# A planned two-branch attention kernel: other times in its plan, one more row place, output products one place later, another table of order

## The chip, the cores and the metric

The kernel runs on one core of a Trainium2 chip. The metric is the device time of one execution in microseconds. The profiler's records of one execution give the span, the busy times and the waits that are quoted below.

## The reference

Two attention layers A and B (own weights, same input `x` of 2048 tokens x 640 features) are computed and mixed with a gate for each token. Each layer has 32 heads of 20 features and works in 4 segments of 512 tokens: causal softmax attention inside the segment (the mask of -1e9 hides a key from the queries ahead of it), plus a read of a memory `M, z` that the earlier segments have filled.

```python
for s in range(N):
    qs, ks, vs = q[:, :, s], k[:, :, s], v[:, :, s]
    logits = jnp.einsum("bhqd,bhkd->bhqk", qs, ks) * scale + mask
    p = _softmax(logits, axis=-1)
    a_dot = jnp.einsum("bhqk,bhkd->bhqd", p, vs)
    pq = phi(qs)
    a_mem = jnp.einsum("bhld,bhde->bhle", pq, M) / (jnp.einsum("bhld,bhd->bhl", pq, z)[..., None] + 1e-6)
    outs.append(g * a_mem + (1.0 - g) * a_dot)
    pk = phi(ks)
    M = M + jnp.einsum("bhld,bhle->bhde", pk, vs)
    z = z + jnp.einsum("bhld->bhd", pk)
...
return g * (a @ wo_A) + (1 - g) * (b @ wo_B)
```

## The kernel before

The eight pairs of segment and layer are numbered `t` = 0 to 7 (`t // 2` is the segment, `t % 2` the layer). For each `t` there are 8 units of four heads, so 64 units `i = 8 t + u`.

**What a unit does.** `s_unit` multiplies queries with keys on TensorE (line 1207); VectorE then scans each block of scores for its row maximum (line 1194), which frees the bank of PSUM that held the block. The maxima are turned into rows on TensorE (`mrow_unit`, line 1232) and sent by DMA into two spare rows of the query tile, so that `t_unit` (line 1297) gets scores with the maximum already taken off. ScalarE takes the exponential (1289), GpSimd cuts the triangle (1290), and `pv_unit` (1317) multiplies with the values. Scores run two units ahead (`LEAD`).

**Fill work.** Between the units TensorE gets products of 640 x 640 weights in split precision: `job_qk`, `job_v`, `job_o`, all through line 771. Each is a list of matmuls of 64 rows on one half of the array, so that two different pieces of work run side by side on the two halves. `window_jobs(t)` writes the list of products that belong to the window of `t`: the remaining q, k and v of `t`, then the first of the five products in `HEAD` of `t + 1` (q0, k0, q1, k1, q2), then the five output products of `t - 1`, then the rest of `HEAD`. PSUM has eight banks, shared by all.

**From the end of a `t` to its output products.** The last `pv_unit` of a `t` sends its rows to memory (`send_dot`). `reciprocals(t, ...)` loads the denominators and gates: line 1377 multiplies them, line 1382 inverts them in two halves of 1.7 us each on VectorE. `mix` loads five blocks of numerators, multiplies each with the inverse (line 1427 on VectorE or 1428 on GpSimd), adds the transposed memory part (1495), and splits the sum into a high and a low part (1418 on ScalarE, 1420 on VectorE or 1421 on GpSimd). Only then can `job_o(t, ...)` run.

**What sets the order.** All engines get an order written ahead by a planner in the kernel: it simulates the engines with a time for each operation (the numbers in `put("D", 0.605, ...)`, `anyof(... D=(...), G=(...))` and `dma(us, ..., lat=...)`), and emits each instruction when its simulated start comes. On the chip each engine runs its list strictly in that order. A time in the plan is thus no wait on the chip; it decides what stands before what, and `anyof` takes the engine with the smaller simulated load. `RULES` holds, for each unit, eight numbers of the planner (order of S and T units, share of the fill, how long units are put off, and so on).

**Rows.** `big` is a pool of 28 places of 128 x 512 f32 in SBUF (`NBIG`) for inputs, split products, probabilities and results. In the last `t`, `fin_unit` used one tile `fin_tmp` of its own.

## Time and profile before

| | |
|---|---|
| Median of 3 runs | 1021.28 us (1020.8 to 1024.54) |
| Profiled execution, own time | 1020.24 us |
| Its span, first to last instruction | 1018.2 us |
| TensorE matmul busy | 1000.0 us, 98% |
| TensorE weight load busy | 857.4 us, 84% |
| VectorE (DVE) busy | 773.7 us, 76% |
| ScalarE (ACT) busy | 659.7 us, 65% |
| GpSimd (POOL) busy | 606.0 us, 60% |
| Granted TensorE clock | 1.000 |

PE is TensorE's matmul row and PEld its weight loads; "busy" is the union over both halves of the array, so a stretch in which only one half works counts as busy in full. A wait row names the engine that waits and its line, then what it waited for, then us in total, the number of times and the longest. Windows give the busy time of each engine in a stretch, with the number of its instructions in brackets.

### The profile page before, as it was taken

To read this page: it belongs to the slowest core of one execution; us is meant where nothing else is said; L and a number is where in the kernel's file an instruction comes from. 1 tells how busy PE (TensorE), PEld (TensorE's weight loads), DVE (VectorE), ACT (ScalarE), POOL (GpSimd) and SP (SyncE) were. 2 spreads that over 40 slices of the span, in tenths; PEclk is the share of its full clock that TensorE was granted. 3 is DMA by queue.
4 is the path that set the end of the run, shared out by engine and by line. 5 is a ranking of instruction groups with operands and counts; after the bars stand their busy time and mean duration, and the time that the engine had idled before them with its cause. 6 is when DMAs were issued, how large, how long until landed. Compare 5 with 4: busy or idle time off the path is not lost.

```text
span 1018.2 us, 30838 instructions
## 1 busy us (share of the span) xinstructions
PE 1000.0 (98%) x11260; PEld 857.4 (84%) x11260; DVE 773.7 (76%) x2611; ACT 659.7 (65%) x1342; POOL 606.0 (60%) x1032
## 2 busy tenths in 40 slices
PE   9899999999999999999999999999999999999998
PEld 7898888878897888878898888988889888888876
DVE  5587876976787768885777977788747887789764
ACT  5276767677775677666765657675676667665672
POOL 4365557756566655766645557486564646557561
PEclk9999999999999999999999999999999999999999
DMA  6998888988997788868768497786976979878531
GB/s 222 299 313 263 272 274 288 289 278 254 263 298 195 253 240 265 249 190 258 230 177 290 130 297 231 223 283 185 279 240 179 310 206 275 243 221 242 133 117 54
DMA packets 148886, 241.99 MB, mean 238 GB/s; under 512 B 13216, under 2 KB 46144, under 8 KB 148416
## 3 DMA queue, kind: packets, MB, share of 16 engines
q1 hardware_dynamic: 148736, 240.03, 76.8%
q8 instruction: 89, 1.46, 0.6%
q14 instruction: 61, 0.50, 0.2%
HBM read 150.83 MB, written 94.65 MB: 241 GB/s over the span
## 4 chain that ended last, share of the span: by engine, by line
PE 84%; DMA 6%; DVE 5%; issue 1%; POOL 1%; ACT 1%; SPq 1%; DVEq 0%; ACTq 0%; POOLq 0%
PE bank L771 48%; PE bank L1317 13%; PE bank L1297 7%; PE bank L1207 7%; PE bank L881 3%; PE bank L963 2%; PE bank L923 2%; DMA dots<-row 1%; DVE bank L1194 1%; DVE row L1420 1%; PE bank L1232 1%; DMA kd<-row 1%; DVE row L1427 1%; DMA qd<-row 1%; DMA kst<-kd 1%
## 5 line engine op out<-in xcount | busy, mean ns | idle before, releaser
L1194 DVE CUSTOM_DVE_ANT_0 bank<-bank,tri 128x512 f32<-128x512 f32 (+3 forms) x1024 | 474.4, 519 | 151.5 <-PE bank L1207 118.6
L771 PE MATMUL bank<-row,wh 64*128 64x512 f32 x2308 | 498.4, 403 | 0.5 <-DVE O L898 0.3
L1289 ACT ACTIVATE p<-bank 128x512 f32<-128x512 f32 x576 | 316.5, 599 | 138.0 <-PE bank L1297 108.9
L1290 POOL TENSOR_SCALAR_AFFINE_SELECT p<-p 128x256 f32<-128x256 f32 (+1 forms) x576 | 219.3, 390 | 224.8 <-ACT p L1289 215.6
L771 PEld LDWEIGHTS bank<-row,wh 64*128 64x128 f32 x2308 | 319.7, 185 | 10.9 <-issue 1.2
L771 PE MATMUL bank<-row,wl 64*128 64x512 f32 x1154 | 297.0, 399 | 0.0
L541 POOL TENSOR_TENSOR wl<-wst,wh 128x640 fp32r<-128x640 f32 x115 | 180.2, 1573 | 65.4 <-ACT wh L539 64.8
L1207 PE MATMUL bank<-kst,qst 60*128 60x384 f32 (+3 forms) x1024 | 177.9, 317 | 4.6 <-DMA kst<-kd 2.8
L1297 PE MATMUL bank<-qst,kst 62*128 62x128 f32 (+3 forms) x1024 | 179.4, 316 | 3.0 <-DVE mx L1194 2.6
L771 PE MATMUL bank<-wvh,row 64*128 64x320 f32 x1280 | 179.8, 315 | 1.1 <-DVE mx L1194 1.1
L771 PEld LDWEIGHTS bank<-row,wl 64*128 64x128 f32 x1154 | 175.0, 186 | 4.1 <-issue 0.2
L771 PEld LDWEIGHTS bank<-wvh,row 64*128 64x128 f32 x1280 | 147.9, 185 | 3.0 <-DVE mx L1194 1.3
L1194 DVE DVE_READ_ACCUMULATOR2_ANT mx<- 128x1 f32 x1024 | 143.4, 140 | 0.0
L1297 PEld LDWEIGHTS bank<-qst,kst 62*128 62x128 f32 x1024 | 134.3, 186 | 9.5 <-DVE mx L1194 3.9
L1317 PE MATMUL bank<-p,vst 128*32 128x256 f32 (+3 forms) x1904 | 142.1, 427 | 0.0
L1207 PEld LDWEIGHTS bank<-kst,qst 60*128 60x128 f32 x1024 | 130.9, 186 | 11.8 <-DMA kst<-kd 2.0
L1317 PEld LDWEIGHTS bank<-p,vst 128*32 128x32 f32 x1904 | 57.8, 110 | 83.4 <-issue 62.5
L539 ACT CAST wh<-wst 128x640 fp32r<-128x640 f32 x119 | 86.1, 741 | 31.6 <-PE bank L771 14.6
L771 PE MATMUL bank<-wvl,row 64*128 64x320 f32 x640 | 100.7, 311 | 0.0
L771 PEld LDWEIGHTS bank<-wvl,row 64*128 64x128 f32 x640 | 80.3, 185 | 0.1
L516 POOL TENSOR_TENSOR wvl<-wst,wvh 128x640 fp32r<-128x640 f32 (+1 forms) x48 | 64.1, 1338 | 25.4 <-ACT wvh L513 15.7
L1347 ACT COPY row<-bank 128x512 f32<-128x512 f32 x56 | 33.1, 590 | 64.4 <-PE bank L1317 59.6
(117 smaller groups left out, 1204.3 us busy)
## 6 DMA issues: line engine op xcount, KB each, us to landing
qst<-qd SPq DMA_DIRECT2D x128, 240.0 KB
kst<-kd SPq DMA_DIRECT2D x128, 240.0 KB
qd<-row SPq DMA_DIRECT2D x40, 512.0 KB
kd<-row SPq DMA_DIRECT2D x40, 512.0 KB
dots<-row SPq DMA_DIRECT2D x56, 256.0 KB
wst<-wmix SPq DMA_DIRECT2D x35, 320.0 KB
row<-dots SPq DMA_DIRECT2D x42, 256.0 KB
qd<-row SPq DMA_DIRECT2D x40, 256.0 KB
```

The costliest lines, as they stand in the source:

```text
L516: put("G", 0.77 * n, lambda: nc.gpsimd.tensor_tensor(out=wl[:, a:b, :], in0=w3, in1=r32(wh[:, a:b, :]), op=ALU.subtract), end, prio=4)
L539: put("A", 0.625, lambda: nc.scalar.copy(wh, w3), lambda: put(lo_eng, lo_cost, lambda: lo.tensor_tensor(out=wl, in0=w3, in1=r32(wh), op=AL ...
L541: lambda: lo.tensor_tensor(out=wl, in0=w3, in1=r32(wh), op=ALU.subtract), end, prio=3), prio=6)
L771: return nc.tensor.matmul(bank_of, lhsT=w[ROWS[half]], rhs=x_[ROWS[half]], start=start, stop=stop)
L881: return nc.tensor.matmul(pm[:, a - h0:c - h0, :].rearrange("p h e -> p (h e)"), lhsT=r32(pqTs[t, m][ROWS[half], P * n:P * (n + 1)]), rhs= ...
L1194: put("D", w / 960.0 + 0.105, lambda: nc.vector.tensor_tensor_reduce(out=sc[:, off:off + w], in0=sc[:, off:off + w], in1=tri[:, L - w:], s ...
L1207: lane_ops[half].append((mm(w), lambda pair=pair, qb=qb, off=off, w=w, r=r, sc=sc: nc.tensor.matmul(sc[:, off:off + w], lhsT=q[r, pair, P ...
L1289: put("A", 0.483, lambda: nc.scalar.activation(pt, sc, AF.Exp, scale=SCALE), lambda: (bank.give(sc), put("G", 0.15 + 0.105 * len(todo), la ...
L1290: "G", 0.15 + 0.105 * len(todo), lambda: nc.gpsimd.affine_select(out=blocks, in_=blocks, pattern=[[0, len(todo)], [1, P]], base=0, channel ...
L1297: lane_ops[half].append((mm(w), lambda pair=pair, kb=kb, off=off, w=w, r=r, sc=sc: nc.tensor.matmul(sc[:, off:off + w], lhsT=k[r, pair, P ...
L1317: nc.tensor.matmul(po[32 * j:32 * j + 32, P * kb:], lhsT=vst[t % 2][:, kb, h * E1:h * E1 + 32], rhs=pts[i, n, f][0][:, off:off + w], start ...
L1347: either(0.483, lambda: nc.scalar.copy(r32(oT), po), 0.605, lambda: nc.vector.tensor_copy(r32(oT), po), end, 2)
```

## The change

The planner gets other times: VectorE's operations with both inputs in SBUF go from 0.605 to 0.85 or 0.9 us, GpSimd's multiply from 1.25 to 1.4, most loads land 0.2 to 0.4 us sooner in the plan (those of the v weights and the token gates too, not shown below), and the score loads of units 0 and 1 land 1.7 us later than they did in it. `big` gets a 29th place, and `fin_unit` takes its temporary from `big`. `window_jobs` puts the output products behind four products of the next `t` instead of three. Nearly all rows of `RULES` are others. No arithmetic changes: both programs hold 9,732 matmuls and 940 DMAs.

```diff
     RULES = {
-        0: "TSTSTSTSTS 1.010 2.38 0.30 8 0.0 1.6 1",
...
+        0: "TSTSTSTSTS 0.933 2.38 0.30 4 0.0 3.08 1",
...
-    def dma(us, emit, then=None, prio=5, lat=1.1, some=False, issue=0.44):
+    def dma(us, emit, then=None, prio=5, lat=0.9, some=False, issue=0.44):
...
-    NBIG, NWST, NWH, SPARE = 28, 3, 4, 2
+    NBIG, NWST, NWH, SPARE = 29, 3, 4, 2
...
         ahead = [(t + 1, kind, m) for kind, m in HEAD] if t < 7 else []
-        got += ahead[:3]
+        got += ahead[:4]
         if t > 0:
             got += [(t - 1, "o", m) for m in range(KT)]
-        got += ahead[3:]
+        got += ahead[4:]
...
-                out=r32(st), in_=xT[P * k:P * (k + 1), L * s:L * (s + 1)]), landed, prio=need[job_index[2 * s, "q", 0]] - 4 * (s > 0), lat=1.6 if s else 1.1)
+                out=r32(st), in_=xT[P * k:P * (k + 1), L * s:L * (s + 1)]), landed, prio=need[job_index[2 * s, "q", 0]] - 4 * (s > 0), lat=1.2 if s else 1.1)
...
                     dma(0.95, lambda dst=dst, src=rows[half], half=half: nc.sync.dma_start(
-                        out=r32(dst[64 * half:64 * half + 3 * DH, :, :]), in_=r32(src)), done, prio=soon)
+                        out=r32(dst[64 * half:64 * half + 3 * DH, :, :]), in_=r32(src)), done, prio=soon, lat=0.9 if i > 1 else 2.8)
...
         def gates():
-            put("D", 0.605, lambda: nc.vector.scalar_tensor_tensor(
+            put("D", 0.9, lambda: nc.vector.scalar_tensor_tensor(
...
-            out=r32(d), in_=lanes_of(t)[:, DH:DH + 1, :].to_broadcast([H, 4, L])), landed, prio=-1, lat=1.6)
+            out=r32(d), in_=lanes_of(t)[:, DH:DH + 1, :].to_broadcast([H, 4, L])), landed, prio=-1, lat=1.2)
...
-                D=(0.605, lambda: nc.vector.tensor_tensor(out=lo, in0=r32(y), in1=r32(hi), op=ALU.subtract)),
+                D=(0.85, lambda: nc.vector.tensor_tensor(out=lo, in0=r32(y), in1=r32(hi), op=ALU.subtract)),
...
-                D=(0.605, lambda: nc.vector.tensor_tensor(out=r32(y), in0=r32(y), in1=r32(r), op=ALU.mult)),
-                G=(1.25, lambda: nc.gpsimd.tensor_tensor(out=r32(y), in0=r32(y), in1=r32(r), op=ALU.mult)))
+                D=(0.9, lambda: nc.vector.tensor_tensor(out=r32(y), in0=r32(y), in1=r32(r), op=ALU.mult)),
+                G=(1.4, lambda: nc.gpsimd.tensor_tensor(out=r32(y), in0=r32(y), in1=r32(r), op=ALU.mult)))
...
-        dma(0.82, lambda: nc.sync.dma_start(out=r32(y), in_=lanes_of(t)[:, 4 * k:4 * k + 4, :]), landed, prio=0, lat=1.6)
+        dma(0.82, lambda: nc.sync.dma_start(out=r32(y), in_=lanes_of(t)[:, 4 * k:4 * k + 4, :]), landed, prio=0, lat=1.2)
...
-    fin_tmp = Store([sb.tile([P, NB, 4, DH], F32, tag=f"ft{i}", name=f"ft{i}", bufs=1) for i in range(1)])
...
-                def got(tmp):
+                def got(row):
+                    tmp = r32(row[:, :4 * NB * DH]).rearrange("p (n h e) -> p n h e", n=NB, h=4)
...
-                fin_tmp.want(1, got)
+                big.want((F32,), got, prio=1)
```

The order of the instructions shows what that moves. First place: TensorE at the start of the program, where the first scores of unit 0 (line 1207, now 1209) stand among the products for v (`wvh`, 128x320). Before:

```order
L771 MATMUL bank_134<-wvh,row_29_204 128x320
L771 MATMUL bank_136<-row_29_204,wh_145 128x512
L1207 MATMUL bank_137<-kst_84,qst_80 128x512
L1207 MATMUL bank_140<-kst_84,qst_80 128x512
L771 MATMUL bank_134<-wvh,row_8_193 128x320
L923 MATMUL bank_135<-ident,row_232_392 128x64 x2
L771 MATMUL bank_134<-wvh,row_15_196 128x320
L923 MATMUL bank_135<-ident,row_232_392 128x64 x2
L771 MATMUL bank_141<-wvh,row_7_192 128x320
L771 MATMUL bank_134<-wvh,row_20_199 128x320
L771 MATMUL bank_141<-wvh,row_14_195 128x320
L771 MATMUL bank_134<-wvh,row_25_202 128x320
```

Now (lines are two further down):

```order
L773 MATMUL bank_134<-wvh,row_20_198 128x320
L773 MATMUL bank_141<-wvh,row_19_197 128x320
L773 MATMUL bank_134<-wvh,row_25_201 128x320
L773 MATMUL bank_141<-wvh,row_24_200 128x320
L773 MATMUL bank_134<-wvh,row_30_204 128x320
L773 MATMUL bank_141<-wvh,row_29_203 128x320
L773 MATMUL bank_134<-wvl,row_7_191 128x320
L773 MATMUL bank_141<-wvh,row_8_192 128x320
L773 MATMUL bank_134<-wvl,row_14_194 128x320
L773 MATMUL bank_141<-wvh,row_15_195 128x320
L1209 MATMUL bank_137<-kst_84,qst_80 128x512
L1209 MATMUL bank_139<-kst_84,qst_80 128x512
```

The two first scores stood ahead of the product with `row_8` of v; now they stand behind sixteen more products (and four transposes, `ident`). The loads they need (`qst_80`, `kst_84`) stand at the same place in the DMA queue as before. The first score of unit 1 likewise stands twelve matmuls later.

Second place: VectorE at the change to `t` = 7, where the inverse of `t` = 6 is made (L1382, now L1384) and its numerators are multiplied (L1427, now L1429). Before:

```order
L737 TENSOR_TENSOR row_17745_15009<-bank_139,row_17744_15008 128x512
L720 TENSOR_SCALAR bank_138<-bank_138 128x512
L1382 RECIPROCAL row_17623_14935<-row_17623_14935 128x256
L721 TENSOR_TENSOR row_17729_15000<-bank_138,row_17729_15000 128x512
L1382 RECIPROCAL row_17623_14935<-row_17623_14935 128x256
L1468 TENSOR_TENSOR fw_15126<-bank_134,gqd 128x16
L1469 RECIPROCAL fw_15126<-fw_15126 128x16
L1470 TENSOR_TENSOR ft_164<-bank_134,fw_15126 128x320
L1427 TENSOR_TENSOR row_17632_14939<-row_17632_14939,row_17623_14935 128x512
L1427 TENSOR_TENSOR row_17635_14940<-row_17635_14940,row_17623_14935 128x512
L1427 TENSOR_TENSOR row_17641_14942<-row_17641_14942,row_17623_14935 128x512
L1194 ISA bank_139,mx_14991<-bank_139,tri 128x384
```

Now:

```order
L1379 SCALAR_TENSOR_TENSOR row_17688_14937<-row_17688_14937,gcol_132,row_17689_14938 128x512
L723 TENSOR_TENSOR row_17778_14992<-bank_137,row_17778_14992 128x512
L1384 RECIPROCAL row_17688_14937<-row_17688_14937 128x256
L1196 ISA bank_136,mx_14999<-bank_136,tri 128x512
L1196 ISA mx_14999 128x1
L1384 RECIPROCAL row_17688_14937<-row_17688_14937 128x256
L1468 TENSOR_TENSOR fw_15134<-bank_134,gqd 128x16
L1469 RECIPROCAL fw_15134<-fw_15134 128x16
L1470 TENSOR_TENSOR row_17926_15111<-bank_134,fw_15134 128x320
L1429 TENSOR_TENSOR row_17700_14942<-row_17700_14942,row_17688_14937 128x512
L1429 TENSOR_TENSOR row_17706_14944<-row_17706_14944,row_17688_14937 128x512
L1196 ISA bank_138,mx_14999<-bank_138,tri 128x384
```

A scan (L1194, now L1196) has come between the two halves of the inverse, and one of the three multiplications has gone to GpSimd. Over the whole program VectorE has 12 of the 35 multiplications instead of 18, and 16 of the 35 subtractions of line 1420 instead of 18.

Third place: the DMA queue (SP) in the window of `t` = 2, where weight tiles (`wst`) are fetched: `wmix` are the weights of the output products of `t` = 1, `in_b_wk` those of k1 of `t` = 3. Before, end of the five output products:

```order
L1165 DMA qst_82<-qd_99 60x2x512 x2
L1165 DMA kst_86<-kd_107 60x2x512 x2
L550 DMA wst_142<-wmix_131 128x5x128
L1033 DMA row_6379_5392<-part_113 128x512
L750 DMA kd_108<-row_6386_5395 128x2x512
L750 DMA kd_108<-row_6387_5396 128x512
L550 DMA wst_144<-in_b_wk_dram 128x640
L1244 DMA qst_80<-mr_163 2x8x128 x2
L550 DMA wst_143<-in_b_wq_dram 128x640
```

Now, their beginning:

```order
L1167 DMA qst_80<-qd_99 60x2x512 x2
L1167 DMA kst_84<-kd_107 60x2x512 x2
L552 DMA wst_142<-in_b_wk_dram 128x640
L552 DMA wst_143<-wmix_131 128x5x128
L552 DMA wst_144<-wmix_131 128x5x128
L1167 DMA qst_81<-qd_99 60x2x512 x2
L1167 DMA kst_85<-kd_107 60x2x512 x2
L552 DMA wst_142<-wmix_131 128x5x128
L1364 DMA dots_119<-row_6224_5233 128x512
```

The weights of k1 came behind the last block of `wmix`; now they come ahead of the first. The output products begin one product later in each window from `t` = 1 to 6.

## The prediction

> **What bounds the kernel now.** I read the page first, then TensorE's waits, then those of its weight loads.

> ```profile
> span 1018.2 us, 30838 instructions
> PE 1000.0 (98%) x11260; PEld 857.4 (84%) x11260; DVE 773.7 (76%) x2611; ACT 659.7 (65%) x1342; POOL 606.0 (60%) x1032
> ```

> TensorE is the bound, and its work does not change. What a new order can win is the 18.2 us in which no matmul ran, and time in which only one half of the array worked, which counts as busy. TensorE's waits, longest first:

> ```profile
> PE bank L1207 <- DMA kst<-kd: 2.8, 2, 1.7
> PE bank L1297 <- DVE mx L1194: 2.6, 3, 1.3
> PE bank L923 <- DVE mx L1194: 2.1, 1, 2.1
> ...
> PE bank L771 <- DVE mx L1194: 1.1, 1, 1.1
> ...
> PE bank L1207 <- DVE mx L1194: 0.6, 2, 0.4
> PE bank L1207 <- DVE mw L895: 0.4, 1, 0.4
> ```

> One wait is for the first key loads; the others, 6.8 us, are all for VectorE, nearly all for banks that its scans (L1194) had not yet freed. The weight loads say the same, and more of it, since a blocked half shows there while the other half still multiplies:

> ```profile
> PEld bank L1297 <- DVE mx L1194: 3.9, 4, 1.8
> PEld bank L923 <- DVE mx L1194: 2.7, 3, 2.3
> ...
> PEld bank L1207 <- DVE mx L1194: 1.8, 5, 0.7
> ```

> These are 8.4 us against 5.3 of the matmul rows of the same lines: 3.1 us in which a half stood still under a busy mark.

> VectorE is 76% busy on average, so the question is where it is late. I looked for stretches in which it worked without a break and hardly on a scan. The windows of L1194 alone (length, VectorE busy with scans, count):

> ```profile
> 432.60:443.10 10.50, 0.06 (x2) 1.00 0.95 279
> 548.60:558.00 9.40, 0.00 (x0) 1.00 0.93 312
> 695.10:704.50 9.40, 0.00 (x0) 1.00 0.78 213
> 913.10:924.70 11.60, 0.06 (x2) 1.00 1.05 333
> 513.90:520.70 6.80, 0.00 (x0) 1.00 0.81 237
> 571.40:578.10 6.70, 0.00 (x1) 1.00 0.71 255
> ```

> Four stretches of 9.4 to 11.6 us, each where one `t` ends and its inverse and mixing fall on VectorE, and two of 6.7 us. What TensorE lost behind them (window, then PE, PEld, DVE, ACT, POOL busy):

> ```profile
> 514.00:524.00 10.00, 10.00 (x135) 8.35 (x134) 8.27 (x23) 3.46 (x9) 2.90 (x6) 1.00 0.74 223
> 572.00:582.00 10.00, 10.00 (x119) 8.95 (x112) 9.45 (x32) 5.39 (x11) 3.01 (x9) 1.00 0.52 185
> ...
> 440.00:450.00 10.00, 9.36 (x85) 7.42 (x87) 9.65 (x33) 5.31 (x10) 5.22 (x9) 1.00 0.61 156
> 552.00:562.00 10.00, 8.69 (x108) 7.66 (x105) 9.84 (x22) 3.51 (x8) 5.20 (x6) 1.00 0.81 248
> 698.00:708.00 10.00, 10.00 (x119) 9.43 (x117) 9.31 (x26) 5.42 (x11) 6.61 (x13) 1.00 0.45 126
> 921.00:931.00 10.00, 7.93 (x106) 7.55 (x103) 10.00 (x23) 4.28 (x8) 7.87 (x6) 1.00 0.93 273
> ```

> The first two windows lie behind the stretches of 6.7 us: TensorE was never idle. Behind the long ones it was idle 0.64 + 1.31 + 0 + 2.07 = 4.0 us. So some 7 us without a scan are covered by the eight banks and the fill work; 9 or more are not, in three cases of four.

> **The change part by part.** The sum is made against the profiled execution's own 1020.24 us; the median shown, 1021.28, is 1.04 above it.

> *First loads later in the plan.* The two `kst` waits of 2.8 us are waits of scores that the plan sent too early. The loads stay where they are in the DMA queue. The first scores of unit 0 now stand behind sixteen more products for v, those of unit 1 behind twelve more matmuls. Such products:

> ```profile
> 24.94 2.06 PE L771 MATMUL bank<-wvh,row 64*128 64x320 f32 x25
> ...
> 26.72 1.01 PE L771 MATMUL bank<-wvl,row 64*128 64x320 f32 x10
> ```

> 25 of them in 1.78 us, 71 ns each: 1.14 us of the first wait (1.7) and 0.85 of the second (1.1) are filled, together 2.0. Bounds: 0, if the maxima of unit 0, now later, hold up its `t_unit` by as much, and 2.8. I take -2.0, since behind it everything is in TensorE's order and moves up.

> *Corrected times of VectorE, with the new table.* The stretch at 913 in the timeline of VectorE, with the scan that ends it:

> ```profile
> 913.02 0.86 DVE L1377 SCALAR_TENSOR_TENSOR row<-row,gcol,row 128x512 f32<-128x512 f32 x1
> 913.81 1.27 DVE L737 TENSOR_TENSOR row<-bank,row 128x512 fp32r<-128x512 f32 x2
> 915.01 0.68 DVE L720 TENSOR_SCALAR bank<-bank 128x512 f32<-128x512 f32 x1
> 915.61 1.74 DVE L1382 RECIPROCAL row<-row 128x256 f32<-128x256 f32 x1
> 917.26 0.62 DVE L721 TENSOR_TENSOR row<-bank,row 128x512 f32<-128x512 f32 x1
> 917.81 1.73 DVE L1382 RECIPROCAL row<-row 128x256 f32<-128x256 f32 x1
> ...
> 920.30 4.57 DVE L1427 TENSOR_TENSOR row<-row,row 128x512 f32<-128x512 f32 x3
> 924.79 0.55 DVE L1194 CUSTOM_DVE_ANT_0 bank<-bank,tri 128x384 f32<-128x384 f32 x1
> ```

> The plan reckoned 3 x 0.605 = 1.8 us for the three multiplications that took 4.49. In the new order a scan stands between the halves of the inverse. Ahead of it are L737 twice, L720, L1377, L721 and one half: 1.27 + 0.68 + 0.86 + 0.62 + 1.74 = 5.2 us; behind it the other half, 0.8 us of small pieces (919.5 to 920.3) and two multiplications at 1.5, 5.5 us. One stretch of 11.6 us becomes two of 5.2 and 5.5. The same sum over the new order at the other three places, with the mean of each line from the trace of before, gives 5.6, 4.9 and 5.6 as the longest; nowhere at a change of `t` is it over 6.4. All are below the 6.7 that cost nothing, so the 4.0 us go: -4.0, bounds 0 and -4.0 (nothing more was idle there).

> The other 6.8 - 4.0 = 2.8 us for VectorE have no single long stretch. There the work itself shrinks:

> ```profile
> L1427 DVE TENSOR_TENSOR row<-row,row 128x512 f32<-128x512 f32 x18 | 18.7, 1072 | 1.5 <-DMA row<-dots 1.5
> L1420 DVE TENSOR_TENSOR row<-row,row 128x512 fp32r<-128x512 f32 x18 | 17.3, 974 | 1.2 <-ACT row L1418 0.9 <-POOL mt L362 0.3
> ...
> L1428 POOL TENSOR_TENSOR row<-row,row 128x512 f32<-128x512 f32 x17 | 25.3, 1498 | 6.0 <-DVE row L1382 5.0 <-DMA row<-dots 0.8
> ```

> Six multiplications and two subtractions leave VectorE, 6 x 1.07 + 2 x 0.97 = 8.4 us, over seven changes of `t` 1.2 us each, which is the size of the waits. I take half, -1.4, bounds 0 and -2.8. GpSimd gets six more at 1.5, 9 us at 60% load; the mixing waits for them, and what covers that is the later output product.

> [...] The row first: multiplications took 4.49 / 3 = 1.5 us each beside GpSimd's own (L1428). [...]

> *The half of the array that stands still.* The 3.1 us shown by the weight loads follow the same waits: -2.0 with two thirds of them, bounds 0 and -3.1.

> *Output products behind four.* One product (15 steps of both halves) is done ahead instead of behind: no work on TensorE, no DMA added, the weight loads of k1 and of the output only change places in SP's queue. It gives the chain from inverse to split sums one product more of time; TensorE's waits have no row for that chain itself (L1420, L1421), so I cost it at 0, bounds 0 and -1.1, the L771 row. What covers it is k1; if k1's weights came late, its wait would be of the size of the key loads.

> *29th place, temporary from the pool.* No wait of TensorE for a row shows; 0, bounds -0.5 and +0.5 (the 0.4 to 0.6 of the smallest rows).

> *New waits.* A new order on all five engines brings its own. The trace cannot show them; its nearest rows are the waits now, 2.8 + 6.8 = 9.6 in all. Between 0 and 9.6 I take +2.0, near the row of one key load, since the new plan's times are nearer to the trace where it was late.

> Sum: 1020.24 - 2.0 - 4.0 - 1.4 - 2.0 + 2.0 = 1012.8; with 1.04 for the median 1013.9, so 1013.9 us.

> **The rivals.**

> *The waits only move.* For: in the windows above VectorE was 9.65 to 10.00 of 10 us busy, so it is full there, and cutting a stretch in two leaves the same work. Then only the first loads and half of the 8.4 us of lighter work count against 2 us of new waits: 1020.24 - 2.0 - 1.4 + 2.0 + 1.04 = 1019.9. Against: in 572 to 582 it was 9.45 busy and TensorE never stopped; what counts is how long a bank waits.

> *Loads later than the plan now thinks: slower.* The plan lets the loads of `reciprocals` and `mix` land 0.4 us sooner. Their readers stand in strictly ordered queues, with scans behind them. If the loads really need the old time, seven loads of seven `t` hold VectorE or GpSimd for 7 x 7 x 0.4 = 19.6 us. All of it on TensorE gives 1013.9 + 19.6 = 1033.5; it decides (over 1026.4) when 12.5 us, two thirds, reach it. The trace has few such waits, which speaks against:

> ```profile
> DVE row L1427 <- DMA row<-dots: 1.5, 1, 1.5
> ...
> ACT row L584 <- DMA row<-in_xT_dram: 5.3, 5, 1.7
> ```

> For it speaks the second row: loads of x do come late, on ScalarE, already with the old time.

> *No new waits and all halves filled.* Every bound on the good side: 1020.24 - 2.8 - 4.0 - 2.8 - 3.1 - 1.1 - 0.5 + 1.04 = 1007.0.

> **How the numbers follow.** A measurement of this kernel tells about 0.5% (5.1 us) from no change. Forecast, 1010 to 1016.1: 0.50. Waits only move, 1016.2 to 1026.4: 0.27. Good ends, below 1010: 0.13. Late loads, slower: 0.10. So faster 0.63, same 0.27, slower 0.10. The likeliest case's own range is 1010 to 1016.1; the range that leaves out no more than 2 in 10 goes from the good ends, 1006 with a little beyond them, to 1021, the upper rival with a little more. The sum's other bound (all gains 0, new waits 9.6) is 1030.9 and lies in the slower case.

> **What would show it.** Right: the `kst` wait of TensorE falls from 2.8 to about 0.8; no stretch without a scan over 7 us at a change of `t`; TensorE's waits for L1194 fall from 6.4 to 3 or less; L1427 has 12 rows. Wrong: stretches below 7 us and yet waits for L1194 of the old size (waits only move), rows of VectorE or GpSimd with a few us for `dots` (late loads), or a new row of TensorE for ScalarE or GpSimd.

## The result and the profile after

| | before | changed |
|---|---|---|
| Median, same chip, 8 executions each | 1022.07 us (1019.83 to 1028.0) | 1015.5 us (1013.68 to 1018.16) |
| Ratio, 95% interval | | 0.9926 (0.9905 to 0.9946) |
| Profiled execution, own time | 1020.24 us | 1016.54 us |
| Its span | 1018.2 us | 1014.8 us |
| Its mean granted clock | 1.000 | 0.995 |

The changed kernel is 6.6 us faster; the forecast was 7.4. The head of its page (both traces hold the same 11,260 matmul records):

```profile
span 1014.8 us, 30827 instructions
PE 1002.1 (99%) x11260; PEld 855.5 (84%) x11260; DVE 769.3 (76%) x2604; ACT 659.5 (65%) x1341; POOL 612.3 (60%) x1040
```

TensorE's waits after, longest first (engine and line that wait, what for, us in total, times, longest; lines are two further down than before):

```profile
PE bank L1234 <- POOL mt L1221: 1.6, 1, 1.6
PE bank L344 <- DVE qst L348: 1.5, 1, 1.5
PE bank L1209 <- DVE row L1349: 0.8, 1, 0.8
PE bank L925 <- DVE row L729: 0.8, 1, 0.8
PE bank L773 <- DVE mw L897: 0.6, 1, 0.6
```

The row for `kst` is gone. No row of a matmul is for a scan (L1196) any more; among the weight loads the largest such row is

```profile
PEld bank L1319 <- DVE mx L1196: 1.1, 4, 0.4
```

where L1297 alone had 3.9. The first row is new and leads to GpSimd and ScalarE; its cause comes below. TensorE in the stretches that the prediction spoke of, and at the start (window, then us and PE, PEld, DVE, ACT, POOL busy, clock, DMA share, GB/s), before:

```profile
0.00:70.00 70.00, 64.80 (x595) 57.48 (x599) 46.33 (x141) 36.21 (x72) 32.71 (x54) 1.00 0.87 272
420.00:460.00 40.00, 37.85 (x435) 33.07 (x433) 34.27 (x101) 26.52 (x54) 26.39 (x40) 1.00 0.70 206
540.00:600.00 60.00, 58.17 (x680) 50.32 (x679) 51.80 (x153) 34.97 (x71) 35.00 (x62) 1.00 0.73 228
680.00:705.00 25.00, 24.88 (x333) 22.47 (x331) 23.27 (x64) 15.46 (x33) 18.18 (x24) 1.00 0.78 236
900.00:950.00 50.00, 47.93 (x561) 40.76 (x561) 46.98 (x148) 32.34 (x67) 33.96 (x53) 1.00 0.72 218
```

and after:

```profile
0.00:70.00 70.00, 67.50 (x644) 60.41 (x646) 46.44 (x147) 39.52 (x79) 34.09 (x58) 1.00 0.92 288
420.00:460.00 40.00, 37.86 (x421) 32.33 (x421) 31.12 (x100) 24.91 (x51) 28.05 (x45) 0.96 0.70 219
540.00:600.00 60.00, 59.12 (x697) 50.40 (x695) 52.90 (x161) 37.17 (x74) 36.05 (x60) 1.00 0.77 232
680.00:705.00 25.00, 24.21 (x259) 19.42 (x257) 22.32 (x74) 14.88 (x30) 17.39 (x23) 0.86 0.64 195
900.00:950.00 50.00, 49.49 (x579) 42.42 (x577) 44.50 (x140) 32.33 (x67) 34.01 (x53) 1.00 0.72 216
```

The start has 2.7 us less idle time, 540 to 600 has 0.95 less, 900 to 950 has 1.56 less. The two others gained nothing: there the clock is 0.96 and 0.86, while it is 1.00 in the windows of before.

**Progress.** All kernels here with the same matmuls can be compared by how far TensorE is in its work. I cut its list into 45 pieces of equal weight (21.5 to 22 us each where nothing disturbs) and read from each trace when a piece ends. The changed kernel leads by 3.2 us after 70 us and by 3.8 at 400. It loses 1.5 at the change from `t` = 2 to 3, wins 1.9 at the next, loses 3.6 at the change from 4 to 5 and wins 0.6 and 1.7 at the last two; 3.4 us remain at the end. "Time in a piece" below is meant so.

**At both losses the clock is halved.** The trace's clock record has the array at half speed for 3.4 us from 438.4 and for 6.8 us from 687.6. After, then before, at the second:

```profile
685.00:690.00 5.00, 4.21 (x35) 3.23 (x34) 5.00 (x11) 3.42 (x7) 4.69 (x5) 0.76 0.93 270
690.00:695.00 5.00, 5.00 (x45) 2.38 (x43) 3.44 (x13) 0.72 (x2) 3.67 (x4) 0.56 0.83 273
```

```profile
685.00:690.00 5.00, 5.00 (x78) 4.87 (x76) 4.32 (x16) 3.24 (x6) 2.19 (x4) 1.00 0.98 322
690.00:695.00 5.00, 5.00 (x65) 4.27 (x65) 4.83 (x21) 2.85 (x7) 4.30 (x7) 1.00 1.02 315
```

After has 35 matmuls where before has 78: the first memory reads (L883, small f32 matmuls) stand without products beside them. PE reads 100% busy at a clock of 0.56; only the count, PEld and the clock tell. At the first loss TensorE is also idle for 1.6 us, of which below. Both places are changes from the first layer of a segment to the second, where the x of the next segment is loaded, and x came later than before: the second row below is of after (before: 5.3).

```profile
DVE row L1379 <- DMA row<-rowg: 5.4, 2, 3.6
ACT row L586 <- DMA row<-in_xT_dram: 9.7, 7, 2.7
```

ScalarE's wait of 2.2 us for the fifth block of x at 436 held up the maxima behind it, which is TensorE's new row of 1.6 us. The first row is the load of the gates for the inverse: at 165 us VectorE stood 3.6 us for it, with scans queued behind. Before, this row was

```profile
DVE row L1377 <- DMA row<-rowg: 0.5, 1, 0.5
```

**How the profiled executions stand to the rest.** Over all comparisons the kernel before ran 66 times, on average 1022.4 us at a mean clock of 0.9956. Four of these had a clock of 1.000 (mean 1019.0 us), twelve had 0.994 (1023.4 us). The profiled execution of before, taken apart from these 66, had 1.000 too; that of after, at 0.995, is ordinary (its eight: 0.9961). So the profiles show 3.7 us of difference between the own times and the medians 6.6.

### The profile page after: what moved, and what is told of

It reads as the page before. It is cut to its first block, busy times and chain, and to the rows that moved or that the text cites. A ratio compares the mean times of both kernels' runs of the same rounds, so it can differ in the third digit from the quotient of the medians.

```text
span 1014.8 us, 30827 instructions
## 1 busy us (share of the span) xinstructions
PE 1002.1 (99%) x11260; PEld 855.5 (84%) x11260; DVE 769.3 (76%) x2604; ACT 659.5 (65%) x1341; POOL 612.3 (60%) x1040
## 4 chain that ended last, share of the span: by engine, by line
PE 84%; DMA 6%; DVE 5%; ACT 1%; POOL 1%; issue 1%; SPq 1%; ACTq 0%; DVEq 0%; POOLq 0%
PE bank L773 50%; PE bank L1319 13%; PE bank L1299 7%; PE bank L1209 7%; PE bank L883 3%; PE bank L965 3%; PE bank L925 2%; DMA row<-dots 1%; DMA dots<-row 1%; DMA kd<-row 1%; DVE bank L1196 1%; PE bank L1234 1%; DVE row L1429 1%; DVE row L1422 1%; DMA row<-in_xT_dram 1%
## 5 line engine op out<-in xcount | busy, mean ns | idle before, releaser
L1196 DVE CUSTOM_DVE_ANT_0 bank<-bank,tri 128x256 f32<-128x256 f32 (+3 forms) x1024 | 474.7, 520 | 150.2 <-PE bank L1209 96.8
L1291 ACT ACTIVATE p<-bank 128x512 f32<-128x512 f32 x588 | 324.0, 601 | 140.0 <-PE bank L1299 108.4
L773 PE MATMUL bank<-row,wl 64*128 64x512 f32 x1154 | 293.3, 402 | 0.0
L1209 PE MATMUL bank<-kst,qst 60*128 60x384 f32 (+3 forms) x1024 | 184.0, 317 | 1.8 <-DVE row L1349 0.8
L1299 PE MATMUL bank<-qst,kst 62*128 62x128 f32 (+3 forms) x1024 | 176.4, 317 | 1.0 <-ACT vst L1015 0.5
L773 PE MATMUL bank<-wvh,row 64*128 64x320 f32 x1280 | 176.7, 312 | 0.0
L1319 PE MATMUL bank<-p,vst 128*32 128x384 f32 (+3 forms) x1936 | 148.9, 431 | 0.0
L1196 DVE DVE_READ_ACCUMULATOR2_ANT mx<- 128x1 f32 x1024 | 144.6, 141 | 0.0
L1209 PEld LDWEIGHTS bank<-kst,qst 60*128 60x128 f32 x1024 | 137.5, 186 | 8.2 <-DVE row L1349 1.2
L1299 PEld LDWEIGHTS bank<-qst,kst 62*128 62x128 f32 x1024 | 130.5, 186 | 7.3 <-DVE mx L1196 1.0
L1349 ACT COPY row<-bank 128x512 f32<-128x512 f32 x61 | 36.0, 590 | 79.4 <-PE bank L1319 71.1
L518 POOL TENSOR_TENSOR wvl<-wst,wvh 128x640 fp32r<-128x640 f32 (+1 forms) x48 | 64.0, 1338 | 17.3 <-ACT wvh L515 17.3
```

The source lines that it names most:

```text
L518: put("G", 0.77 * n, lambda: nc.gpsimd.tensor_tensor(out=wl[:, a:b, :], in0=w3, in1=r32(wh[:, a:b, :]), op=ALU.subtract), end, prio=4)
L773: return nc.tensor.matmul(bank_of, lhsT=w[ROWS[half]], rhs=x_[ROWS[half]], start=start, stop=stop)
L1196: put("D", w / 960.0 + 0.105, lambda: nc.vector.tensor_tensor_reduce(out=sc[:, off:off + w], in0=sc[:, off:off + w], in1=tri[:, L - w:], s ...
L1209: lane_ops[half].append((mm(w), lambda pair=pair, qb=qb, off=off, w=w, r=r, sc=sc: nc.tensor.matmul(sc[:, off:off + w], lhsT=q[r, pair, P ...
L1291: put("A", 0.483, lambda: nc.scalar.activation(pt, sc, AF.Exp, scale=SCALE), lambda: (bank.give(sc), put("G", 0.15 + 0.105 * len(todo), la ...
L1299: lane_ops[half].append((mm(w), lambda pair=pair, kb=kb, off=off, w=w, r=r, sc=sc: nc.tensor.matmul(sc[:, off:off + w], lhsT=k[r, pair, P ...
```

## The experiments

"Plan untouched" means that the planner reckons as in the changed kernel (or in the kernel before) and only what it emits differs, so the order on the other engines stays. Ratios are to the kernel before on the same chip, with 95% intervals.

**First loads as before, in the changed kernel.**

```diff
-  ... done, prio=soon, lat=0.9 if i > 1 else 2.8)
+  ... done, prio=soon)
```

> The changed kernel with the plan's landing time of the score loads of units 0 and 1 put back to the common 0.9 us; the table stays. In its order the first score of unit 0 stands 25 matmuls earlier than in the changed kernel. My theory (about 3 us of the gain are the start): TensorE waits again for the key loads, 2.5 us or more, and reaches the work that the changed kernel reached at 60 us some 3 us later. Rival (the start is hidden, the gain is the table's): no such wait, same progress at 60 us. The whole time is less sure, since the order behind the start is another one too, with a longest stretch without a scan of 13.9 us at one change of t: 1018 to 1024.

Measured: 1049.61 us, 1.0268 (1.0220 to 1.0316). The start is 1.8 us later after 70 us and 2.3 us later after 92 us than in the changed kernel, but the wait for the keys that was expected, 2.5 us or more, did not come:

```profile
PE bank L1209 <- DMA kst<-kd: 0.3, 1, 0.3
```

So this run does not show that the later start is the keys' wait. The other 32 us are those of another order on all engines.

**VectorE's times as before, in the changed kernel.**

```diff
-  put("D", 0.9, ...    D=(0.85, ...    D=(0.9, ...   G=(1.4, ...
+  put("D", 0.605, ...  D=(0.605, ...   D=(0.605, ...  G=(1.25, ...
```

> The changed kernel with the old plan times of the VectorE and GpSimd operations on rows (0.605 and 1.25). The order sends 21 multiplications to VectorE instead of 12, and the longest stretches without a scan at the seven changes of t are 6.8, 9.2, 4.6, 7.1, 8.6, 3.9, 4.8 us. My theory (long stretches stop TensorE): TensorE waits for VectorE again behind the stretches of 9.2 and 8.6, 3 to 4 us in all, the start stays fast: 1016 to 1020. Rival (only the sum of VectorE's work counts): all waits for VectorE grow alike, at all changes of t.

Measured: 1074.45 us, 1.0508 (1.0456 to 1.0561). The waits for scans are back:

```profile
PE bank L925 <- DVE mx L1196: 2.4, 2, 1.6
PE bank L1299 <- DVE mx L1196: 1.7, 2, 1.4
PE bank L773 <- DVE mx L1196: 1.5, 1, 1.5
```

and the clock is at half speed for some 60 us in all, in seven places. The direction agrees with the theory; the size is again that of an order to which the table does not fit.

**Another order of no meaning** (one number of the table).

```diff
-  8: "TSTSTSTSTS 0.989 2.39 0.30 8 0.0 0.78 1",
+  8: "TSTSTSTSTS 1.010 2.39 0.30 8 0.0 0.78 1",
```

> The changed kernel with one number of the table put back for one unit (unit 8: 0.989 becomes 1.010), which says nothing about the chip but gives another order of some 17% of the places from unit 8 on. It measures how far an order alone moves the time. My theory: the start as in the changed kernel, and within 4 us of it, 1012 to 1020. Rival (the gain is the luck of this one order): back to 1020 or more.

Measured: 1050.66 us, 1.0281 (1.0239 to 1.0322). One number of one unit, without any meaning for the edits, costs 35 us. The rival holds: the gain hangs on this one order. So an edit cannot be judged by undoing it in the planner: the two runs above measure mostly the lost fit. How much of the gain is the table's own, and how much that of the corrected times, no run here separates. All that follow leave the plan untouched.

**Filling TensorE ahead of the memory reads.**

```diff
         b = bank.free.pop(0)
+        if t in (3, 5):
+            for _ in range(1):
+                nc.tensor.matmul(b, lhsT=tri[:, :P], rhs=tri, start=True, stop=True)
```

> The changed kernel with one extra matmul (128x512 bf16 on the whole array, its result overwritten) ahead of each of the 16 memory reads (line 883) of t = 3 and t = 5; order otherwise the same. The profile of the changed kernel shows the granted clock at half speed for 3.4 us at 438 and for 6.8 us at 688, each time after a stretch of small memory reads and transposes; half of 10.2 us is 5.1 us lost. My theory (too little work in the array, though the matmul row is busy, lowers the clock): the two dips are gone, 5.1 us won against 16 x 0.23 = 3.7 us of extra work, 1012 to 1016. Rival (the dips have to do with something else, such as a wait): they stay, and the time is 3.7 us longer, 1019.

Measured: 1021.18 us, 0.9997 (0.9975 to 1.0019). At 688 us the clock stayed whole and the piece took 24.2 us instead of 27.8, but at 433 us it was halved for 6.8 us instead of 3.4, with the same filling; and the sixteen matmuls took 389 ns each in the trace, not the 0.23 us that the expectation reckoned with. What halves the clock stays open.

**x earlier.**

```diff
+            if s and k == KT - 2:
+                nc.sync.dma_start(out=r32(gw[:, :L]), in_=xT[P * (k + 1):P * (k + 2), L * s:L * (s + 1)])
+            own = s > 0 and k == KT - 1
+            src = gw[:, :L] if own else st
...
-            dma(0.87, lambda: nc.sync.dma_start(
+            dma(0.87, (lambda: None) if own else lambda: nc.sync.dma_start(
```

> The changed kernel with its plan untouched, but the fifth block of x of segments 1 to 3 is fetched some 15 to 20 us earlier, into the tile of the gate weights, which rest then (they are fetched again afterwards, two more loads). Every order but the DMA queue's stays word for word. Theory (late x, as a mechanism that took back part of the gain): ScalarE's wait for x at 436 us and at 691 us goes, with it TensorE's wait of 1.6 us on the maxima behind it, and the two stretches of halved clock (3.4 us at 438 and 6.8 us at 688, which cost about 1.7 and 3.4 us) go with the idle time that precedes them: 2 to 6 us faster than the changed kernel, ratio to the kernel before 0.986 to 0.991. Rival (the halved clock comes from the dense small matmuls and transposes at a change of segment, not from x): only the 1.6 us, ratio about 0.991, the clock still dips at 438 and 688. Second rival (only the fit of the whole order counts): the two extra loads and moved transfers bring new waits, ratio 0.995 or more.

Measured: 1015.64 us, 0.9925 (0.9905 to 0.9946). At 435 to 440, after and then here:

```profile
435.00:440.00 5.00, 3.41 (x24) 2.69 (x24) 3.84 (x12) 3.92 (x9) 3.48 (x6) 0.84 0.66 229
```

```profile
435.00:440.00 5.00, 4.96 (x47) 4.48 (x47) 4.79 (x15) 3.95 (x9) 5.00 (x7) 1.00 0.56 180
```

The wait and the halved clock at this place went together, and the piece took 24.2 us instead of 27.3: there the theory holds. At 687 us the clock fell as before, although x was there: for this place the rival holds. The time as a whole did not move; a piece at 345 us took 1.7 us longer, behind a weight load on which ScalarE waited 1.6 us.

**All multiplications on VectorE.**

```diff
-  G=(1.4, lambda: nc.gpsimd.tensor_tensor(out=r32(y), in0=r32(y), in1=r32(r), op=ALU.mult)))
+  G=(1.4, lambda: nc.vector.tensor_tensor(out=r32(y), in0=r32(y), in1=r32(r), op=ALU.mult)))
```

> The changed kernel with its plan untouched, but the 23 multiplications of the numerators that GpSimd had are issued on VectorE, at the same places of the order. VectorE gets 23 x 1.07 to 1.29 = 25 to 30 us more work, spread between scans (longest stretch without a scan about 7 us), GpSimd loses about 34 us. Prediction's term (8.4 us less work on VectorE taken as 1.4 us, bounds 0 and 2.8): 25 to 30 us more are worth 4 to 5 us, bounds 0 and 10, so ratio to the kernel before about 0.997, range 0.992 to 1.002. [...]

Measured: 1023.86 us, 1.0009 (0.9989 to 1.0028), some 8.5 us above the changed kernel's ratio, toward the far end of the prediction's bounds. The groups of VectorE in the changed kernel (count, then busy us and mean ns of one):

```profile
L1422 DVE TENSOR_TENSOR row<-row,row 128x512 fp32r<-128x512 f32 x16 | 18.2, 1148 | 0.0
L1429 DVE TENSOR_TENSOR row<-row,row 128x512 f32<-128x512 f32 x12 | 15.3, 1291 | 0.0
```

and here:

```profile
PE 1005.3 (98%) x11260; PEld 860.5 (84%) x11260; DVE 778.5 (76%) x2627; ACT 659.1 (65%) x1341; POOL 579.5 (57%) x1017
L1430 DVE TENSOR_TENSOR row<-row,row 128x512 f32<-128x512 f32 x23 | 17.2, 746 | 0.0
L1422 DVE TENSOR_TENSOR row<-row,row 128x512 fp32r<-128x512 f32 x16 | 15.3, 968 | 0.0
L1429 DVE TENSOR_TENSOR row<-row,row 128x512 f32<-128x512 f32 x12 | 11.7, 992 | 0.0
```

VectorE has 23 multiplications more and only 9.2 us more work: without GpSimd's multiplications beside them the other 28 went from 33.5 to 27.0 us. The time is not lost evenly: of the 6.0 us between the two traces, 4.0 are lost at the last change of `t` (at most 1.7 of them to 3.4 us of half clock at 931), where VectorE works 6.8 us without a scan and TensorE has a new wait for an eviction that stands behind the multiplications:

```profile
PE bank L1299 <- DVE row L729: 3.6, 1, 3.6
```

**The inverse three times, twice, not at all.** The first of these edits (`c` is 0 for the first half and 1 for the second); the second has `1 + c` in place of `1 + 2 * c`, and the third leaves both halves out:

```diff
-  put("D", 1.78, lambda: nc.vector.reciprocal(r32(d[:, cols]), r32(d[:, cols])),
+  put("D", 1.78, lambda: [nc.vector.reciprocal(r32(d[:, cols]), r32(d[:, cols])) for _ in range(1 + 2 * c)],
```

> The changed kernel with its plan untouched, but the second half of each inverse is computed three times in a row (the inverse of the inverse of the inverse, the same value). VectorE gets 7 x 3.5 = 24.4 us more work, about as much as in the run with all multiplications on VectorE, but all of it inside one stretch for each change of t: the longest stretch without a scan goes from 6.2, 6.4, 5.6, 4.9, 5.6, 5.2, 5.2 us to about 9.5, 6.4, 8.9, 5.0, 6.2, 5.2, 7.8 for t = 0 to 6. Theory (what counts is the longest stretch; over 9 us it costs 0.6 to 2 us, under 7 nothing): 1 to 4 us slower than the changed kernel, at the changes of t = 0, 2 and 6, nothing at the other four; ratio 0.993 to 0.997. Rival (total work of VectorE counts): spread over all seven changes, as much as in the other run, 4 us or more.

> The changed kernel, its plan untouched, with the second half of each inverse computed twice (that half then holds the denominators again, so the output is not the reference's): 7 x 1.74 = 12.2 us more work for VectorE at the changes of t. Without the inverse the changed kernel was 2 us faster (24.4 us less work), with it made three times 27 us slower (24.4 us more). If TensorE pays for every microsecond that is added there (no slack left at any change): half of 27, about 13 us slower, 1028 to 1030, ratio 1.006. If there is a slack of 1 to 2 us at each change, beyond which it pays in full: 0 to 6 us slower, 1016 to 1022, ratio 0.993 to 0.999.

> The changed kernel, its plan untouched, without its inverse (both halves left out, output not the reference's). Theory: it gains less than the kernel before does from the same cut, since its shorter stretches have already taken part of it: 4 to 12 us faster than the changed kernel, ratio to the kernel before 0.981 to 0.988; the distance of the two kernels without inverse is 2 to 4 us instead of 7. Rival (the changed kernel's gain has nothing to do with VectorE at the changes of t): the distance stays at 6 to 8 us. Second rival (nothing to earn there): ratio 0.990 to 0.993, as with the inverse.

Measured: three times 1042.75 us, 1.0189 (1.0163 to 1.0214); twice 1025.66, 1.0035 (1.0020 to 1.0050); not at all 1013.18, 0.9900 (0.9872 to 0.9927). TensorE's waits with the inverse three times:

```profile
PE bank L1299 <- DVE row L729: 6.3, 3, 2.8
PE bank L1209 <- DVE O L900: 3.7, 2, 3.5
PE bank L1209 <- DVE row L729: 2.9, 1, 2.9
PE bank L773 <- DVE row L1470: 2.6, 1, 2.6
PE bank L1209 <- DVE mx L1196: 2.5, 1, 2.5
PE bank L773 <- DVE mx L1196: 2.5, 1, 2.5
```

One wait of 2.5 to 3.5 us at each of the seven changes of `t`, five of the seven for evictions (L729, L900, L1470) and two for scans. The time in the pieces at the changes:

| inverse | `t` = 0 | 1 | 2 (two pieces) | 3 (two) | 4 | 5 | 6 |
|---|---|---|---|---|---|---|---|
| none | 21.4 | 22.1 | 50.7 | 43.8 | 28.5 | 21.7 | 23.5 |
| once | 22.3 | 23.3 | 50.7 | 44.4 | 27.8 | 21.8 | 24.4 |
| twice | 23.8 | 25.1 | 48.2 | 47.7 | 29.1 | 23.3 | 26.1 |
| three times | 24.9 | 26.9 | 51.5 | 49.6 | 32.1 | 26.0 | 27.9 |

The table holds the clock too: with the inverse three times it is halved for 3.4 us at `t` = 3 and at `t` = 5, where the changed kernel's is whole (at most 1.7 us of each loss), and twice was faster at `t` = 2 because its clock stayed whole there.

The theory of the longest stretch falls: it expected nothing at `t` = 1, 3, 4 and 5, and 3.6, 5.2, 4.3 and 4.2 us were lost there. By the trace the longest stretches without a scan are 5.8, 6.6 and 6.3 us at `t` = 3, 4 and 5; at `t` = 1 it is 8.2 us, as in the changed kernel, and not the stretch that was lengthened. Twice is nearer to "every microsecond is paid": 10 us for 12.2 us of work. Of the 27 us for three times, a part is the clock's: its four executions have 0.9885 on average, the changed kernel's eight 0.9961. In the other direction almost nothing is earned, as the second rival said: 24.4 us less work, 2.3 us less time; the two intervals leave room for anything from nothing to some 6 us.

**No inverse in the kernel before.**

```diff
-  put("D", 1.78, lambda: nc.vector.reciprocal(r32(d[:, cols]), r32(d[:, cols])),
+  put("D", 1.78, lambda: None,
```

> The kernel before, its plan untouched, without its inverse (line 1382 is not issued in either half; the numerators are multiplied with the denominators themselves, so the output is not the reference's). VectorE loses 14 x 1.74 = 24.4 us of work, 3.5 us at each of the seven changes of t. In the run with the inverse made three times, 3.5 us more cost 3.9 us at each change. Theory (VectorE's queue at the change of t is on the path that sets the end, in both kernels, and more so before): the kernel before gains 10 to 18 us here, ratio 0.982 to 0.990, and it comes within 2 to 4 us (what the start is worth) of the changed kernel without its inverse. Rival (more work there delays, less earns nothing, because other waits stand right behind): less than 4 us gained, ratio above 0.996.

Measured: 1017.61 us, 0.9945 (0.9927 to 0.9963): 5.6 us, between the theory and its rival and nearer the rival. So all the work of the inverse, taken off VectorE, is worth 5.6 us in the kernel before. It does not bound what cutting the stretches is worth, since the order of the scans stayed: the four long stretches have still no scan for 10.2, 9.7, 9.5 and 12.1 us (432, 544, 692 and 909 us), and TensorE still waits 3.9 us for scans, instead of 6.4:

```profile
PE bank L923 <- DVE mx L1194: 2.6, 1, 2.6
...
PE bank L1297 <- DVE mx L1194: 0.9, 1, 0.9
...
PE bank L1207 <- DVE mx L1194: 0.4, 1, 0.4
```

Without the inverse the distance of the two kernels is 0.0045 of 1022 us, 4.6 us, instead of 7.6 by the ratios; with intervals of 2 to 3 us each this suggests, and does not show, that some 3 us of the gain hang on it.

**Both repairs together.** x early for segment 2 alone, and the filling matmul for `t` = 5 alone.

> The changed kernel, its plan untouched, with the two repairs that each gained where it was made: the fifth block of x is fetched early for segment 2 alone (the stretch around 438 us took 24.2 us instead of 27.3 then), and one 128x512 matmul that feeds nothing stands ahead of each of the eight memory reads of t = 5 (the stretch around 688 us took 24.2 us instead of 27.8 then). If both gains stand side by side: 5 to 6.5 us faster than the changed kernel, about 1009 to 1010.5, ratio 0.987 to 0.989, no halved clock before the end. If they were luck of one execution: 0.992 as the changed kernel.

Measured: 1017.61 us, 0.9943 (0.9921 to 0.9965), not below the changed kernel. The gain at 438 us came again (24.7 us for the piece), the one at 688 us did not: the clock was halved there for 6.8 us in spite of the filling matmuls. None of the kernels that compute the whole output was clearly faster than the changed kernel.

**The first keys without their wait, in the kernel before.**

```diff
+  src_ = rows[half] if i > 1 else xs[0, 0][0][:3 * DH, None, :].to_broadcast([3 * DH, 2, L])
-  dma(0.95, lambda dst=dst, src=rows[half], half=half: ...
+  dma(0.95, lambda dst=dst, src=src_, half=half: ...
```

> The kernel before, its plan and the places of all loads untouched, but the loads of the first queries and keys (units 0 and 1) take their 60 rows from the split input in SBUF instead of from memory, so that they need not wait for the queries and keys to be written there (the scores of these two units are wrong, so is the output). It measures the prediction's first term alone. Theory (the two waits for the first keys, 2.8 us, are paid in full, since all behind them is in TensorE's order): 2.5 to 3.2 us faster, about 1019 to 1020, ratio 0.997; the first 50 us come to within 0.5 us of the changed kernel's. Rival (the wait covers another one right behind it): under 1 us.

Measured: 1022.36 us, 1.0007 (0.9994 to 1.0019): no gain. The windows at 30 to 35 us, of the kernel before, here, and of the changed kernel:

```profile
30.00:35.00 5.00, 3.05 (x36) 2.49 (x35) 1.42 (x4) 1.91 (x4) 1.68 (x2) 1.00 1.06 358
```

```profile
30.00:35.00 5.00, 3.83 (x45) 3.47 (x46) 2.78 (x9) 1.02 (x2) 1.05 (x1) 1.00 1.01 362
```

```profile
30.00:35.00 5.00, 5.00 (x67) 5.00 (x66) 1.69 (x5) 1.04 (x3) 1.07 (x1) 1.00 1.03 395
```

One wait for keys of 1.0 us stayed, yet this kernel was 2.9 us ahead of before after 48 us and still 2.0 ahead at 270. Of that 1.0 was left at 450, and stretches of halved clock at 559 and 928 turned the rest round. The theory holds for the first 50 us and fails for the time, where the rival (under 1 us) came true; what consumed the lead between 300 and 450 us isn't settled.

## Why the prediction came out right, point by point

- **First loads, -2.0.** In the trace the start won 3.2 us (idle 5.2 to 2.5 us up to 70 us). Larger than taken, since the waits for the keys went whole and not to the 0.8 us that should have been left. The run with this edit undone starts 1.8 to 2.3 us later, but with a wait for the keys of only 0.3 us, so it does not show that they are the reason. But the reason given, that all behind it moves up, did not hold in the kernel before: a lead of 2.9 us at the start was worth nothing at the end. How much of the 3.2 us is in the 6.6 is open.
- **Long stretches of VectorE, -4.0.** 2.5 us came: 0.95 at 548 and 1.56 at 913, where the prediction had 1.31 and 2.07. At 432 and 695 the idle time stayed or grew (0 and +0.67), with late x and the halved clock there. In these two the inverse does not lie in the stretch of before, as the prediction had it: it was made at 420 and 679 us, and mixing and memory reads fill the stretch. The step that failed is the threshold, "some 7 us without a scan are covered": with the inverse repeated, TensorE lost 4.2 to 5.2 us, and waited 2.5 to 3.5 us at a time, at three changes where no stretch exceeds 6.6 us. The length of the longest stretch thus does not tell what is covered; the banks that wait stand behind the inverse in VectorE's order, two of these three for an eviction and one for a scan. Where the inverse is made, two stretches above 7 us remain, the longer one at `t` = 0:

```profile
165.30:175.60 10.30, 0.00 (x0) 1.00 0.97 273
286.30:294.40 8.10, 0.00 (x0) 1.00 0.91 329
911.80:916.70 4.90, 0.00 (x0) 1.00 1.04 366
```

  (Windows of L1196 alone in the changed kernel. In the first VectorE stands 3.6 us for the gates' load, in the second, at `t` = 1, it is idle for 2.1 us; the third was 11.6 us long before.) A third, at 692 us and behind the inverse, is just over 7 (7.1 us). So "nowhere over 7 us" missed clearly at two changes of seven, both by waits of VectorE that a sum of durations leaves out.
- **VectorE's lighter work, -1.4.** VectorE's busy time fell by 4.4 us, not by 8.4. The eight operations fewer of L1427 and L1420 saved 36.0 - 33.5 = 2.5 us, since the remaining ones rose from 1072 to 1291 ns and from 974 to 1148. In the run with all multiplications on VectorE the other 28 operations gave back 6.5 of the 17.2 us that the 23 added, and in the time these 23 cost 8.5 us. What six are worth cannot be read from that, since two thirds of the loss lie at one change of `t`; there TensorE waits 3.6 us for an eviction that stands behind the multiplications (L1299 for L729), where in the changed kernel, with 23 of them on GpSimd, all waits of that row come to 0.3 us.
- **Half of the array, -2.0.** The weight loads' rows for scans fell from 3.9, 2.7, 1.8 us to at most 1.1. The time of this alone wasn't measured.
- **Output products behind four, 29th place, 0.** Nothing in the traces speaks for them. Undone in the planner they would be measured through another order, so they weren't tried.
- **New waits, +2.0.** They came in another kind than reckoned: one row of 1.6 us and 10.2 us of half clock, at most 5.1 us of work; the largest of the waits now is well under the 9.6 us allowed. In the medians this does not count against the change, as the kernel before suffers as much in its ordinary executions (mean clock 0.9956 before and 0.9961 after). The profiled execution of before, from which the sum started, was 2 us better than its kernel is on average, and the 1.04 us that the prediction added covered half of that.
- **The rivals.** "The waits only move" is right that a cut in two leaves VectorE as tight as it was (every added microsecond is still paid) and wrong that TensorE gains nothing. "Loads later than the plan": both of its rows appeared, 5.4 us on VectorE and 9.7 on ScalarE instead of 0.5 and 5.3, but TensorE felt 1.6 us and, by the run with x earlier, one halved clock of it, far from the 12.5 that would have decided.

The forecast of 1013.9 thus has the right sum from terms of which the largest was too big (4.0 for 2.5) and the start too small (2.0 for 3.2); the two errors partly cancelled, and that is luck. So is the base: between the two profiled executions, to which the terms belong, the change won 3.7 us and not 7.4; that of before lost nothing to the clock, that of after up to 5.1 us. What the 6.6 us of the medians are made of stays open in part: a lead of 2.9 us at the start was worth nothing in the kernel before, some 3 us seem to hang on the inverse's work, and the table's share is not measured.

## What to carry to other kernels

In a program whose order is planned, test an edit with the plan held fixed and only the emission changed; undoing it in the planner measures the lottery of another order (here 35 us for one number). Slack at a tuned place is one-sided: ask with one run of added and one of removed work, since here a microsecond more cost about a microsecond, where a microsecond less earned a tenth (in the kernel before a quarter). And look at the granted clock of many executions before a profiled one is used as the base of a sum.
